# A planned attention-plus-FFN kernel: new load sizes in the planner, a new order of the first loads, value loads held to a short backlog

## The chip, the core and the metric

The kernel runs on one core of a Trainium2 chip. The metric is device time in microseconds (us) of one launch; three runs of the kernel before took 354.30, 354.94 and 356.14 us, median 354.94. The profile shows one execution of its own (354.98 us, of which 353.2 us is the span that the profile covers) at a granted TensorE clock of 1.00.

## What is computed

Attention over 8 batches, 12 heads, 448 positions of 64 values, with q and k normalised, and then a feed-forward block on the 3584 resulting rows of 768:

```
q_n, k_n = rmsnorm(q, g_q), rmsnorm(k, g_k)
attn     = softmax(q_n @ k_n.T / sqrt(64))          # 448 x 448 per head
x        = (attn @ v), heads side by side           # 3584 x 768
a, b     = x @ w1, x @ w2                           # 3584 x 1024 each
out      = ((a * b) @ w3) @ w_out                   # 3584 x 768, float32
```

All inputs are float32 in DRAM. The weights are not normalised or gated further, so w3 @ w_out can be multiplied once, ahead of use.

## The kernel before

**Work units.** The unit of attention is a quad: four heads of one batch, 24 in all (`i` = 0 to 23, three to a batch). For each quad:

- q and k are loaded (two transfers of 448 KB; quads 1 to 5 on GpSimd's queue, the others on SyncE's), squared on ScalarE (L455), summed on VectorE (L462), turned into a scale on ScalarE (L471, L474) and scaled to bf16 on VectorE (L485). Quads 0 to 4 are then transposed on TensorE (L1112), the others by DMA transposes from SyncE (L552).
- Seven score steps (L670) of four matmuls each go to two PSUM banks; each is followed by one exponential on ScalarE (L692), which writes the `P` or `Pr` tile. A planned order never has more than two scores waiting for their exponential.
- The values are loaded by four small GpSimd transfers (L399, 64 and 48 KB), and the products with them (L736, L757), together with products with ones for the softmax sum, are done for two quads at a time where possible ("pair") or for one ("single"). ScalarE makes the reciprocal (L779, L780), VectorE scales into `xT` (L799).

The feed-forward part works in "pairs": two PSUM banks, two halves of the contraction on the two row halves of the array. The w3·w_out product is 8 such pairs (128 passes of four 64x64 matmuls, 384 columns), w1 and w2 are 64 pairs (768 passes, 448 columns), the last product is 27 pairs (432 passes, 384 columns) and a shorter tail (L1053). All of these are issued at one line, L857. In the middle of each pair the two row halves swap banks, and an empty instruction (L841) on GpSimd, or early on SyncE, carries the wait for that: the pair's second half can start only when the queue of that engine has reached it.

**How the order is made.** Nothing is scheduled on the chip. When the kernel is built, class `Planner` plays the work through, with a duration in us for each piece, and emits every engine's instructions in the order that came out. At run time each engine takes its instructions strictly in that order, and waits for data where it must. What the change touches in this planner:

- *The loads.* A transfer has a size in us (`moves=(work, weight)`): two queues, SyncE's and GpSimd's, are played as sharing the DMA engines by weight, each finishing its transfers in turn. 0.7 us (`AFTER`) is added for a landing, and `LATE` more after 75 us.
- *`plan.moving["SP"]`*: what SyncE's queue still has to move at 2.3 us, for quad 0's q and k.
- *`POOL_ORDER`*: the order of the first 27 loads on GpSimd's queue: `w` is a 128-row slab of w3 (512 KB read), `o` a quarter of w_out, `q` a quad's q and k, `v` a quad's values (four transfers), `a` and `b` a third of w1 and w2 (1 MB read).
- *`quiet()`*: holds a quad's value load back while the load queue has more than `QUIET` us left, unless its scores are due.
- *`PARTS`*: in how many steps of the contraction the first three w3·w_out pairs alternate between their sides (each step needs only the quarters of w_out that have come).
- *`HOLD`*: with 1, a pair product with the values isn't started while a feed-forward pair is open and no other is ready. *`STOCK`* and *`PACE`*: with that many feed-forward pairs waiting, scores are spaced by 1.7 us.
- Where TensorE would idle before 13 us, the planner puts matmuls on zeros (L1182, 256 columns) [...].

Of the kernel before, what the change touches and what calls it, by code (L numbers as in the profile page):

```python
# [19 lines left out]
INF = float("inf")  # L20
# [4 lines left out]
LAG = {"ACT": 0.11, "DVE": 0.09, "SP": 0.0, "POOL": 0.0}  # L25
AHEAD = {"SP": 2.0, "POOL": 1.6}
AFTER = 0.7
LATE = 1.0
BUSY = 75.0


# [164 lines left out]
def kernel(  # L196
# [48 lines left out]
    MARGIN = 0.25  # L245
    LOW = 2
    PV_BANKS = 6
    HOLD = 1
    SOON = 0
    STARVED = 4  # L250
    HUNGRY = 0.6
    ONE = 0
    PARTS = ((4, 8), (4, 8), (4, 8))
    EARLY_PAIRS = 3
    AHEAD_W3 = 4
    EARLY = 4
    STOCK = 18
    PACE = 1.7
    POOL_ORDER = (
        "w0 o0 o1 w1 w2 o2 o3 q1 v0 w3 w4 q2 v1 a0 w5 w6 a1 v2 w7 v3 q3 a2 q4 b0 b1 q5 b2".split()  # L260
    )
    ON_POOL = (1, 2, 3, 4, 5)
    IN_PARTS = (6, 7, 8)
    QUIET = 0.5

    w1s = const.tile([128, CM, DFF], BF, name="w1s")
    w2s = const.tile([128, CM, DFF], BF, name="w2s")
# [46 lines left out]
    plan = Planner()  # L314
# [27 lines left out]
    def put(where, key):  # L342
        def done(t):
            where[key] = t

        return done
# [23 lines left out]
    def plan_load_qk(i, key=None):  # L370
        eng, queue = (nc.gpsimd, "POOL") if i in ON_POOL else (nc.sync, "SP")
        parts = 2 if i in IN_PARTS else 1
        for which in range(2):
            got = []

            def done(t, which=which, got=got):
                got.append(t)
                landed[i]["qk"[which]] = all_of(got, parts)

            for n in range(parts):  # L380
                x0, x1 = 2 * n // parts, 2 * (n + 1) // parts
                add(
                    queue, {"SP": 0.4, "POOL": 0.75}[queue],
                    (QUAD * i - 30 if key is None else key) + which * 0.01 + n * 0.001,
                    lambda which=which, x0=x0, x1=x1: load_qk(i, which, eng, x0, x1),
                    needs=[lambda: qk_free[i % 3] + (1.0 if i > 5 else 0.0)],
                    done=done, moves=(1.4 / parts, 0.086),
                )

    def load_v(i, z):  # L390
# [15 lines left out]
    def plan_load_v(i, key):  # L406
        got = []

        def done(t):
            got.append(t)  # L410
            if len(got) == 4:
                landed[i]["v"] = max(got)

        def quiet():

            late = i <= 3 or next_score[0] >= i * NU - 3
            return 0.0 if late or sum(x[1] for x in plan.moving["SP"]) < QUIET else INF

        for z in range(4):
            add(  # L420
                "POOL", 0.62, key + z * 0.01, lambda z=z: load_v(i, z),
                needs=[lambda: v_free[i % 4] + (3.0 if i > 3 else 0.0), quiet], done=done,
                moves=((0.48, 0.06), (0.40, 0.05))[z % 2],
            )

    def load_w12(dst, src, m):
# [860 lines left out]
    with tc.manual_schedule():  # L1287
        nc.vector.memset(warm_t, 0.0)
        nc.vector.memset(eps_t, 64e-6)
        nc.vector.memset(ones, 1.0)  # L1290
        nc.vector.memset(ones[HP:NP, 1], 0.0)
        nc.vector.memset(ones[0:HP, 2], 0.0)
        nc.vector.memset(ones_row, 1.0)
        for which in range(2):
            load_qk(0, which, nc.sync, 0, 1)
            load_qk(0, which, nc.scalar, 1, 2)
        nc.scalar.dma_start(out=g_row[:, 0], in_=g_q.unsqueeze(0))
        nc.scalar.dma_start(out=g_row[:, 1], in_=g_k.unsqueeze(0))
        nc.scalar.preload_act_table_set("natural_log_exp_and_others")
        make_identity(nc, ident)  # L1300
        for t_sb in v_bufs:
            nc.gpsimd.memset(t_sb[:, :, NF, :], 0.0)  # L1302
        def warm(n):
            for _ in range(n):
                nc.tensor.matmul(
                    out=ps_all[:, 7, :], lhsT=warm_t[:, 0:128], rhs=warm_t,
                    start=True, stop=True,
                )

        def g_product():  # L1310
            nc.vector.scalar_tensor_tensor(
                out=gp_row,
                in0=g_row[:, 0].unsqueeze(1).broadcast_to([1, 2, D]),
                scalar=8.0,
                in1=g_row[:, 1].unsqueeze(1).broadcast_to([1, 2, D]),
                op0=MULT, op1=MULT,
            )
            nc.tensor.matmul(
                out=ps_all[:, 6, 0:D], lhsT=ones_row, rhs=gp_row[:, 0],
                start=True, stop=True,  # L1320
            )
            nc.tensor.matmul(
                out=ps_all[:, 6, D : D + 1],
                lhsT=gp_row.rearrange("a x d -> a (x d)"), rhs=ones_row[:, 0:1],
                start=True, stop=True,
            )
            warm(1)

        def spread():
            nc.vector.tensor_copy(out=g_b, in_=ps_all[:, 6, 0:D])  # L1330
            nc.vector.tensor_copy(out=g_col, in_=ps_all[:, 6, D : D + 1])

        warm(WARM)
        free.update(ACT=4.0, DVE=4.0, SP=4.0, POOL=2.3, PE=7.2)
        plan.now = plan.moved_to = 2.2
        plan.moving["SP"].append([2.3, 2.6, lambda t: None, 0.086])
        landed[0].update(q=4.5, k=5.4)
        bank_at[6] = INF
        add(
            "DVE", 0.13, -13.0, g_product, needs=[lambda: 5.8], done=put(consts_at, "gp")  # L1340
        )
        add(
            "DVE", 0.22, -11.0, spread, needs=[lambda: consts_at["gp"] + 0.6],
            done=lambda t: consts_at.update(g=t + SEM) or bank_at.__setitem__(6, t + SEM),
        )
        for i in range(3):
            plan_prep(i)

        seq = [0]

        def weight(emit, moves, done):
            add("POOL", 0.6, -100.0 + seq[0], emit, done=done, moves=moves)

        for name in POOL_ORDER:
            what, x = name[0], int(name[1])
            seq[0] += 1
            if what == "o":
                weight(lambda x=x: load_wout(x), (2.15, 0.135), put(w_at["w_out"], x))
            elif what == "w":
                weight(lambda x=x: load_w3(x), (1.38, 0.172), put(w_at["w3"], x))  # L1360
            elif what == "v":
                plan_load_v(x, -100.0 + seq[0])
            elif what == "q":
                plan_load_qk(x, -100.0 + seq[0])
            else:
                dst, src, key = (w1s, moe_w1, "w1") if what == "a" else (w2s, moe_w2, "w2")
                weight(
                    lambda dst=dst, src=src, x=x: load_w12(dst, src, x), (2.6, 0.323),
                    put(w_at[key], x),
                )  # L1370
        waiting.extend(w34_pair(fc) for fc in range(CF))
        plan.run(pe_step, finished)
        if PLAN_OUT is not None:
            PLAN_OUT.append(dict(free))
# [28 lines left out]
```

## Time and profile before

| what | value |
|---|---|
| time, median of 3 | 354.94 us |
| span of the profiled execution | 353.2 us |
| TensorE (PE) matmuls | 7370, busy 98% of the span |
| ScalarE (ACT) | busy 261.1 us, 74% |
| VectorE (DVE) | busy 206.5 us, 58% |
| GpSimd (POOL) | busy 76.8 us, nearly all of it issuing transfers |
| DMA | 55.11 MB, mean 156 GB/s |

How to read it: "busy" of TensorE counts each matmul from issue to the end of its drain, and four small matmuls run side by side, so a row of the group list with a mean of 349 ns doesn't mean that one matmul follows the other after 349 ns. What counts is the distance from start to start, which the chain of waits and the timeline give: 14 passes of four matmuls in 2.65 us, 0.189 us each. In the last 70 us TensorE alone works: ScalarE and VectorE fall to two tenths, so whatever moves the end has to move TensorE's stream.

### The profile page before, as it was taken

What the parts mean: (1) busy time and instruction counts of PE and PEld (TensorE: products, weight loads), DVE (VectorE), ACT (ScalarE), POOL (GpSimd) and SP (SyncE); (2) the same over time, 40 slices, a digit from 0 to 9 for tenths busy, and PEclk for the clock granted to TensorE, in tenths of its full rate; (3) what the DMA queues carried; (4) which work ended last, traced back from release to release, by engine and by line L of the source; (5) the groups of instructions that cost most, each with busy time, mean ns of one, the idle gap of its engine ahead of it and who ended that gap; (6) DMA issues with size and microseconds to landing.
All of it is one profiled execution on the core that took longest, in us unless ns stands there. A gap on an engine that the chain in (4) does not pass through costs nothing.

```text
span 353.2 us, 16174 instructions
## 1 busy us (share of the span) xinstructions
PE 344.5 (98%) x7370; PEld 220.8 (63%) x7370; DVE 206.5 (58%) x292; ACT 261.1 (74%) x376; POOL 76.8 (22%) x134
## 2 busy tenths in 40 slices
PE   8899999999999999999999999999999999999995
PEld 4566756666665666667666565665656567666674
DVE  5359478897979487987767696576344320122200
ACT  5569979979989999999998999695979612222132
POOL 8365722211220403032032240230400000000000
PEclk9999999999999999999999999999999999999999
DMA  8999999598998999998999889783580005100046
GB/s 189 233 270 189 212 254 297 136 186 203 196 241 175 197 159 246 196 201 171 212 232 207 158 127 256 189 94 56 91 153 2 4 2 136 48 4 2 10 132 178
DMA packets 68488, 55.11 MB, mean 156 GB/s; under 512 B 45060, under 2 KB 62372, under 8 KB 68420
## 3 DMA queue, kind: packets, MB, share of 16 engines
q1 hardware_dynamic: 49440, 35.33, 44.7%
q0 software_dynamic: 18048, 16.92, 28.3%
q10 hardware_dynamic: 932, 1.84, 1.5%
q8 instruction: 57, 0.93, 1.1%
q14 instruction: 11, 0.09, 0.1%
HBM read 46.66 MB, written 11.01 MB: 163 GB/s over the span
## 4 chain that ended last, share of the span: by engine, by line
PE 87%; ACT 6%; DMA 2%; POOL 2%; issue 2%; DVE 1%; POOLq 0%; SPq 0%; ACTq 0%
PE ps_all L857 62%; PE ps_all L757 12%; PE ps_all L670 8%; ACT P L692 3%; PE ps_all L736 2%; DMA w_outs<-in_moe_w_out_dram 2%; ACT half L692 1%; POOL v_sb L399 1%; PE ps_all L1112 1%; PE ps_all L1053 1%; ACT Pr L692 1%; PE ps_all L1182 0%; DVE abT L938 0%; ACT qkT L350 0%; POOL v_sb L1302 0%
## 5 line engine op out<-in xcount | busy, mean ns | idle before, releaser
L692 ACT ACTIVATE P<-ps_all 128x896 bf16<-128x896 f32 x114 | 99.1, 922 | 9.7 <-PE ps_all L670 9.6
L399 POOL DMA_DIRECT2D v_sb<-in_v_dram x96 | 57.2, 609 | 176.8 <-PE ps_all L670 84.6
L857 PE MATMUL ps_all<-xT,w1s 64*64 64x448 bf16 x1536 | 89.4, 349 | 0.0
L857 PE MATMUL ps_all<-xT,w2s 64*64 64x448 bf16 x1536 | 88.0, 349 | 0.4 <-POOLq L841 0.4
L857 PE MATMUL ps_all<-w34s,abT 64*64 64x384 bf16 x1728 | 80.5, 323 | 0.1
L350 ACT ACTIVATE half<-ps_all 128x896 bf16<-128x896 f32 (+1 forms) x40 | 34.8, 869 | 56.1 <-PE ps_all L857 56.1
L938 DVE TENSOR_TENSOR abT<-ps_all,half 128x896 bf16<-128x896 f32 x32 | 34.8, 1089 | 57.3 <-PE ps_all L857 56.8
L857 PEld LDWEIGHTS <-abT 64*64 64x64 bf16 x1728 | 52.2, 107 | 19.6 <-POOLq L841 0.5
L857 PEld LDWEIGHTS <-w2s 64*64 64x64 bf16 x1536 | 47.6, 107 | 25.3 <-POOLq L841 0.8
L857 PEld LDWEIGHTS <-w1s 64*64 64x64 bf16 x1536 | 46.1, 107 | 25.5 <-issue 0.2
L670 PE MATMUL ps_all<-qkT 64*64 64x448 bf16 x672 | 60.9, 352 | 0.9 <-ACT P L692 0.4
L462 DVE TENSOR_REDUCE ssq<-sq 128x14 f32<-128x896 f32 (+1 forms) x50 | 51.2, 1041 | 13.9 <-ACT sq L455 13.9
L485 DVE TENSOR_TENSOR qks<-qk_sb,al 128x448 bf16<-128x448 f32 x96 | 55.5, 617 | 1.4 <-ACT al L474 1.1
L455 ACT ACTIVATE sq<-qk_sb 128x896 f32<-128x896 f32 (+1 forms) x50 | 45.3, 917 | 1.6 <-DMA qk_sb<-in_q_dram 1.5
L799 DVE TENSOR_TENSOR xT<-ps_all,r 128x448 bf16<-128x448 f32 x48 | 27.4, 617 | 12.7 <-ACT r L780 10.1
L670 PEld LDWEIGHTS <-qkT 64*64 64x64 bf16 x672 | 21.7, 106 | 14.9 <-issue 5.1
L857 PE MATMUL ps_all<-w_outs,w3T 64*64 64x384 bf16 x512 | 24.9, 324 | 1.6 <-DMA w_outs<-in_moe_w_out_dram 1.0
L692 ACT ACTIVATE w_outs<-ps_all 128x896 bf16<-128x896 f32 x24 | 21.5, 915 | 5.3 <-PE ps_all L670 5.1
L757 PE MATMUL ps_all<-P,v_sb 128*32 128x448 bf16 x456 | 25.0, 352 | 0.0
L692 ACT ACTIVATE Pr<-ps_all 128x896 bf16<-128x896 f32 x24 | 22.3, 929 | 1.7 <-PE ps_all L670 1.6
L757 PEld LDWEIGHTS <-v_sb 128*32 128x32 bf16 x592 | 15.8, 97 | 12.2
L356 DVE COPY half<-ps_all 128x768 f32<-128x768 f32 x9 | 8.6, 956 | 22.0 <-PE ps_all L857 14.0
(66 smaller groups left out, 214.8 us busy)
## 6 DMA issues: line engine op xcount, KB each, us to landing
out_dram<-half SPq DMA_DIRECT2D x48, 192.0 KB, 3.5
qk_sb<-in_q_dram SPq DMA_DIRECT2D x15, 448.0 KB, 5.3
qk_sb<-in_k_dram SPq DMA_DIRECT2D x15, 448.0 KB, 5.8
v_sb<-in_v_dram POOLq DMA_DIRECT2D x48, 64.0 KB, 3.9
v_sb<-in_v_dram POOLq DMA_DIRECT2D x48, 48.0 KB, 4.2
qk_sb<-in_q_dram POOLq DMA_DIRECT2D x5, 448.0 KB, 8.3
qk_sb<-in_k_dram POOLq DMA_DIRECT2D x5, 448.0 KB, 10.1
w3s<-in_moe_w_dram POOLq DMA_DIRECT2D x8, 256.0 KB, 7.5
```

What stands on the lines that cost most here:

```text
L350: nc.scalar.activation(out=out, in_=in_, func=AF.Copy, scale=1.0 if by is None else by)
L356: nc.vector.tensor_copy(out=out, in_=in_)
L399: nc.gpsimd.dma_start(out=v_bufs[i % 4][p0 : p0 + HP, g::2, 0 : j1 - j0].rearrange("p h j d -> p h (j d)"), in_=src[:, g::2, j0:j1].rearra ...
L455: nc.scalar.activation(out=s["sq", t][:, x0:x1], in_=src[:, t, x0:x1], func=AF.Square)
L462: nc.vector.tensor_reduce(out=s["ssq"][:, t, x0:x1], in_=s["sq", t][:, x0:x1], axis=AX, op=ADD)
L485: nc.vector.tensor_tensor(out=s["qks"][:, t, :, x], in0=src[:, t, x], in1=s["alpha"][:, t, x].unsqueeze(2).broadcast_to([NP, NJ, D]), op=MULT,
L670: nc.tensor.matmul(out=sc[HP * c : HP * c + HP, u, 0:S].rearrange("p (j s) -> p j s", j=NJ), lhsT=qkT[u * D : (u + 1) * D, 1, j, cols], rh ...
L692: lambda: nc.scalar.activation(out=dst, in_=sc[:, :, 0:S], func=AF.Exp),
L757: nc.tensor.matmul(out=ps_all[hd * HALF : (hd + 1) * HALF, z, 0:S], lhsT=value_weights(i, hd, j, kind), rhs=s["P"][:, hd, j, :] if j < NF ...
L799: lambda: nc.vector.tensor_tensor(out=xT[b][:, 2 * m + kind - 1, :], in0=ps, in1=s["r"], op=MULT),
L857: mm = nc.tensor.matmul(out=ps_all[64 * h : 64 * h + 64, p.bank + z, 0 : p.n], lhsT=lhsT[64 * r : 64 * r + 64, 64 * h : 64 * h + 64], rhs= ...
L938: nc.vector.tensor_tensor(out=abT[bp][:, f0 : f0 + 2, odd * S : (odd + 1) * S], in0=ps_all[:, z : z + 2, 0:S], in1=a_sb[b, f0], op=MULT,)
```

## The change

The planner's load sizes are set to other values (w_out 2.15 to 1.95, w3 1.38 to 1.27, w1/w2 2.6 to 2.7, q and k 1.40 to 1.35, values 0.48/0.40 to 0.28/0.24, what is left of quad 0's at the start 2.6 to 3.5), the added lateness after 75 us falls from 1.0 to 0.3 us, the first loads get another order (a quarter of w_out first, w3's slabs earlier, w1 later), and a value load now waits for both queues to be short, GpSimd's own as well as SyncE's, so that values go out a few at a time. Three settings of the planner change with it. The intent is an order that fits when data arrives. What is computed is the same, and so are the instructions of the work itself; only their order, and the number of matmuls on zeros, differ.

```diff
-LATE = 1.0
+LATE = 0.3
...
-    HOLD = 1
+    HOLD = 0
...
-    PARTS = ((4, 8), (4, 8), (4, 8))
+    PARTS = ((2, 4, 8), (4, 8), (4, 8))
...
-    STOCK = 18
+    STOCK = 14
...
-        "w0 o0 o1 w1 w2 o2 o3 q1 v0 w3 w4 q2 v1 a0 w5 w6 a1 v2 w7 v3 q3 a2 q4 b0 b1 q5 b2".split()
+        "o0 w0 w1 w2 o1 o2 o3 q1 v0 w3 w4 w5 q2 v1 v2 w6 w7 a0 a1 v3 a2 q3 q4 b0 b1 q5 b2".split()
...
-    QUIET = 0.5
+    FIRST = 3.5
+    QUIET = 1.0
...
-                    done=done, moves=(1.4 / parts, 0.086),
+                    done=done, moves=(1.35 / parts, 0.086),
...
-            return 0.0 if late or sum(x[1] for x in plan.moving["SP"]) < QUIET else INF
+            left = [sum(x[1] for x in plan.moving[e]) for e in ("SP", "POOL")]
+            return 0.0 if late or max(left) < QUIET else INF
...
-                moves=((0.48, 0.06), (0.40, 0.05))[z % 2],
+                moves=((0.28, 0.06), (0.24, 0.05))[z % 2],
...
-        plan.moving["SP"].append([2.3, 2.6, lambda t: None, 0.086])
+        plan.moving["SP"].append([2.3, FIRST, lambda t: None, 0.086])
...
-                weight(lambda x=x: load_wout(x), (2.15, 0.135), put(w_at["w_out"], x))
+                weight(lambda x=x: load_wout(x), (1.95, 0.135), put(w_at["w_out"], x))
-                weight(lambda x=x: load_w3(x), (1.38, 0.172), put(w_at["w3"], x))
+                weight(lambda x=x: load_w3(x), (1.27, 0.172), put(w_at["w3"], x))
-                    lambda dst=dst, src=src, x=x: load_w12(dst, src, x), (2.6, 0.323),
+                    lambda dst=dst, src=src, x=x: load_w12(dst, src, x), (2.7, 0.323),
```

## Prediction

> **What bounds the kernel now.** I read the page first, its engines and its slices.
>
> ```profile
> PE 344.5 (98%) x7370; PEld 220.8 (63%) x7370; DVE 206.5 (58%) x292; ACT 261.1 (74%) x376; POOL 76.8 (22%) x134
> ...
> PE   8899999999999999999999999999999999999995
> ...
> ACT  5569979979989999999998999695979612222132
> ```
>
> TensorE never rests, and after about 280 us ScalarE is down to two tenths. So the end moves only if TensorE's stream gets shorter or waits less. How much waiting is in it? Busy time doesn't tell, since small matmuls overlap. I priced the stream from starts, with two lines of the chain of waits:
>
> ```profile
> 191.34 2.65 PE ps_all L857 x56
> ...
> 281.60 63.44 PE ps_all L857 x1424
> ```
>
> The first is 14 passes of four matmuls, 0.189 us each; 384-column passes take 0.1625 by the same reading. The stream: 768 passes of w1/w2 145.3, 432 of the last product 70.2, 128 of w3·w_out 20.8, 168 of scores 31.8, value products 49.2 (864 matmuls on whole rows at 0.189 per four, 288 on half rows at 0.69 per 24), 134 transposes at 0.056 7.5, tail 2.6, 18 matmuls on zeros at 0.109 2.0: about 329.3. To this come 66 changes between kinds of matmul (0.09 each beyond the normal step: 5.9). From 7.2 us, where the work starts, that ends at 342.5; the last matmul really ends at 349.4. **So TensorE waits 6.9 us in all**, and that is everything an order can win. Counting the stream up to each value product and comparing with its start in the chain (24.3, 44.7, 75.2, 277.3 us and so on), 3.0 are lost before the first (24.2 us), 0.6 more to the second (44.7), 0.6 to 75, 2.2 to 277, 0.5 in the tail.
>
> The waits of TensorE and its timeline say on what:
>
> ```profile
> PE ps_all L857 <- DMA w_outs<-in_moe_w_out_dram: 1.0, 1, 1.0
> PE ps_all L670 <- ACT P L692: 0.4, 2, 0.2
> PE ps_all L670 <- ACT Pr L692: 0.4, 1, 0.4
> PE ps_all L857 <- POOLq L841: 0.4, 1, 0.4
> ```
>
> ```profile
> 8.56 0.56 PE L1112 MATMUL ps_all<-ident,qks 128*128 128x128 bf16 x7
> 10.14 0.52 PE L857 MATMUL ps_all<-w_outs,w3T 64*64 64x384 bf16 x8 [1.01 <-DMA w_outs<-in_moe_w_out_dram]
> ...
> 118.10 0.38 PE L670 MATMUL ps_all<-qkT 64*64 64x448 bf16 x4 [0.23 <-ACT P L692]
> ...
> 118.91 0.38 PE L670 MATMUL ps_all<-qkT 64*64 64x448 bf16 x4 [0.43 <-ACT Pr L692]
> ...
> 205.05 3.58 POOL L399 DMA_DIRECT2D v_sb<-in_v_dram  x6 [2.03 <-issue]
> ...
> 207.21 1.33 PE L857 MATMUL ps_all<-xT,w2s 64*64 64x448 bf16 x24 [0.40 <-POOLq L841]
> ...
> 345.13 1.12 PEld L857 LDWEIGHTS <-abT 64*64 64x64 bf16 x32 [0.50 <-POOLq L841]
> ```
>
> (Each shown gap is about 0.17 short of the lost time, since the drain of the matmul before counts as busy.) The first quarter of w_out came 1.0 us after the order wanted it. At 118 four scores stand in a row and wait for exponentials. At 207 the swap instruction sat in GpSimd's queue behind six value loads. At 345 the last pair has no partner to fill its swap.
>
> **What the Trainium skill says.** "TensorE: Matmul & The Clock Gate", Back-to-back issue gap, gives N/2.4 + 2.5 ns from start to start: 189 and 162.5 ns; the trace agrees (0.189). "Perfetto Trace Analysis", Identifying the Most-Contended Engine, warns that matmul busy time is no measure of headroom; here 98% hides 6.9 us. "DMA: Bandwidth & Descriptors", Issuing engines are not separate DMA queues: transfers from all engines interleave on the same 16. The trace agrees: beside quad 0's loads from SyncE and ScalarE (landed by 5.4 us) GpSimd's first two landed only at 7.0 and 10.1, later ones come 1.25 (w3) and 1.87 us (w_out) apart. Same page, Anatomy of one DMA: about 2.0 us of fixed time; the fastest value loads here land 2.2 us after issue.
>
> **The change, part by part.** The built order has the same 1536 + 1536 + 1728 + 672 + 512 + 888 work matmuls and the same 11 pair and 2 single products, so no work goes away. Zeros rise from 18 to 22 (+0.44), changes of kind fall from 66 to 63 (-0.27): counted, the new stream ends at 342.6 against 342.5. The rest is waits.
>
> *Start (load order, sizes, FIRST, PARTS).* Landings in the trace before: w0 6.97, o0 10.10, o1 11.98, w1 13.23, w2 14.52, o2 16.37, o3 18.26, q1/k1 21.00, v0 21.96, w3 23.18. The old planner expected the first ones earlier and the later ones late (2.15 for a w_out quarter that takes 1.87). Re-timed in the new order by those steps: o0 about 8.2, w0 10.1, w1 11.35, w2 12.6, o1 14.5, o2 16.4, o3 18.3, v0 unchanged. The new TensorE order, counted: first w3 transposes at 10.3 (in time), the second at 10.9 (0.45 late), the third at 12.75 (in time). With o0 alone 8 passes can run (PARTS gives the first pair four of them); the ninth falls at 14.6, o2 is wanted at 18, o3 at 19: all in time. Lone pair halves before the first value product cost 0.5 before (0.26 + 0.27) and I keep that. Loss 1.0 (0.5 to 2.0) for 3.0; the first value product at 22.3 instead of 24.2, with v0 there when needed.
>
> *22 to 45.* The new order does 16 more w3·w_out passes here (2.6 us that no longer follow the second value product). Scores of quads 1 and 2 start later, about 31.4 instead of 28.4, and 13.3 us of stream stand between them and the second value product; ScalarE has 14 x 0.83 + about 1.5 = 13.1 us in it. That just fits. Loss 0.7 (0.3 to 1.5) for 0.6.
>
> *45 to 75.* The queue delivers the same bytes, so b2 lands near 61.6 as before. The new order runs the first w2 half in one piece (24 matmuls) where the old stopped after 16; its last 8 fall at about 62.4. Quad 3's transposes stand together at about 52, and its q and k (43.0 and 44.1 before) come behind a2 now, near 46 and 47. Squares, sums and scaling take 5 us: up to 1 us of wait. Loss 1.1 (0.3 to 2.5) for 0.6.
>
> *75 to 280.* Before, one run of four scores (lost 1.0) and the GpSimd queue at 207 and 216 (0.8) are the main losses. The new order has no run of four but two of three; the third can't start before the first's exponential is done, 0.6 each. The longest run of value loads ahead of a swap falls from nine to seven, at 0.60 us each 4.2 for 5.4 us. What waits behind them is the swap, and TensorE behind it; this is the one wait the change could still leave. Fewer loads at once cost nothing, since a quad's values land many us before their product. LATE and the smaller sizes move q, k and transposes' uses up to 0.7 us earlier. ScalarE waited only 1.5 us in all for q and k before, so most of that is slack. Loss 1.8 (1.0 to 4.0) for 2.2.
>
> HOLD, STOCK and PACE only choose which ready piece TensorE takes next; what they cost or bring is already in the counted order, at nothing but these waits.
>
> *Tail.* Twelve halves of the last product follow the last w2 half, so six pairs can go two by two and none stands alone: 0.2 for 0.5.
>
> Sum: 342.6 + 1.0 + 0.7 + 1.1 + 1.8 + 0.2 = 347.4 against 349.4: **2.0 us less**, 354.94 - 2.0 = 352.9.
>
> **Rivals.** (1) *Better throughout*: every stage at its lower end (2.1 us of waits): 344.7, so 4.7 less, 350.2. For it: only data and swaps are waited for. Against: two planned score runs. (2) *The start's gain is taken back*: ScalarE, 9.28 of 10 us busy between 30 and 40, fixes the second value product, and late quad 3 and b2 eat the rest: waits 6.5, 349.1, 354.6. (3) *Slower*: the planner now believes in landings that come later. If 0.4 of the 0.7 us taken from LATE reaches TensorE for 10 of the 15 quads loaded after 75 us, that is 4 us, on top of the main sum 351.4: 356.9. For it: loads of q and k took 3.3 to 7.2 us from issue to landing there, a wide spread. Against: the 1.5 us.
>
> **How the numbers follow.** Main case 0.47, rival 1 0.12, rival 2 0.23, rival 3 0.18. The likeliest is 352.9. The range takes in rival 1 and rival 3 and is open a little at both: 349.6 to 357.2. Faster by over 0.5% means under 353.17: rival 1 and most of the main case, 0.53. Slower, above 356.7: most of rival 3 and a little else, 0.18. The same: 0.29.
>
> **What would show it.** Right: no wait for w_out at 10 us, first value product near 22.3, the second with all w3·w_out done near 45.6; no wait for POOLq over 0.3 us between 75 and 280; no half alone at the end. Wrong: waits for DMA on q, k or transposes after 75 us; a stop near 52 or 62 us over 1 us; three-score runs that cost over 1 us each.

## The result, and the profile after

| | before | after |
|---|---|---|
| time, median (lowest to highest) | 355.5 us (354.3 to 356.1, 6 runs) | 358.6 us (357.4 to 361.5, 6 runs) |
| span of the profiled run | 353.2 us | 358.3 us |
| TensorE's last end in it | 349.4 us | 354.3 us |

The kernel after takes 1.010 of the time of before (95% interval 1.0057 to 1.0144): 3 us more, where 2 us less were predicted. It was profiled twice (the second time is called e9 below), and the two profiles differ: TensorE ends at 354.3 in the first, of a 360.1 us execution, and at 352.5 in the second, of a 358.6 us execution, which is the more typical one.

The page of the first, its engines and two of its slices:

```profile
PE 346.2 (97%) x7374; PEld 235.0 (66%) x7374; DVE 208.3 (58%) x294; ACT 261.2 (73%) x374; POOL 76.7 (21%) x134
...
PE   8998899999999999999999999999999999999995
...
ACT  4776797999999999988789898776696933222122
```

TensorE is as full as before and ScalarE as empty after 280 us, so again only TensorE's own stream and its waits can have moved the end. The stream didn't. From the chain of waits of after:

```profile
240.99 1.89 PE ps_all L859 x40
...
292.44 59.05 PE ps_all L859 x1336
```

Ten passes of four matmuls in 1.89 us are 0.189 each, as before, and the same work ends at the same counted 342.6 us. So TensorE waits 354.3 - 342.6 = 11.7 us in the first profile and 9.9 in the second, against 6.9 before; the prediction had 4.8. (Line numbers in after are one or two higher: L857 is L859 here, L670 L672, L455 L457.) TensorE's waits in the first profile:

```profile
PE ps_all L1136 <- DMA w3s<-in_moe_w_dram: 1.9, 3, 1.0
PE ps_all L1307 <- DVE warm_t L1290: 1.2, 1, 1.2
PE ps_all L859 <- issue: 1.2, 2, 0.9
PE ps_all L738 <- ACT w_outs L694: 0.7, 2, 0.4
PE ps_all L672 <- ACT qkT L351: 0.7, 1, 0.7
PE ps_all L672 <- ACT P L694: 0.7, 1, 0.7
```

The w_out wait of before is gone (the L1307 line is the warm-up at 1 us, in every profile). In its place stand the transposes of w3, 1.9 us; "issue", a stop for which the profile shows no releaser; and scores that waited for ScalarE. Where the first and the last of these come from shows in ScalarE's and GpSimd's rows. ScalarE's waits for q and k, before and then after:

```profile
ACT sq L455 <- DMA qk_sb<-in_q_dram: 1.5, 3, 0.7
```

```profile
ACT sq L457 <- DMA qk_sb<-in_q_dram: 4.0, 3, 2.5
ACT sq L457 <- DMA qk_sb<-in_k_dram: 3.5, 4, 2.0
```

1.5 us have become 7.5. L457 computes the squares of a quad; everything behind it in ScalarE's order, exponentials too, waits along. But when these waits fall matters, since LATE acts only after 75 us. Before that time they are 5.1 us (1.2 in the kernel before), most of it in two places, quad 1's q and quad 2's k:

```profile
20.32 0.95 ACT L457 ACTIVATE sq<-qk_sb 128x896 f32<-128x896 f32 x1 [2.53 <-DMA qk_sb<-in_q_dram]
...
30.29 0.95 ACT L457 ACTIVATE sq<-qk_sb 128x896 f32<-128x896 f32 x1 [2.00 <-DMA qk_sb<-in_k_dram]
```

From 75 us on they are 2.4 us in this profile and 3.7 in the second, against 0.3 before. Now the timeline of after between 30 and 38 us, GpSimd and TensorE:

```profile
30.55 0.59 POOL L400 DMA_DIRECT2D v_sb<-in_v_dram  x1 [2.36 <-DMA qk_sb<-in_k_dram]
31.14 1.12 POOL L435 DMA_DIRECT2D w3s<-in_moe_w_dram  x2
...
35.74 0.62 PE L1136 MATMUL ps_all<-ident,w3s 128*128 128x128 bf16 x8 [0.61 <-DMA w3s<-in_moe_w_dram]
...
37.31 0.62 PE L1136 MATMUL ps_all<-ident,w3s 128*128 128x128 bf16 x8 [0.95 <-DMA w3s<-in_moe_w_dram]
```

GpSimd wants to issue the last of the eight value loads of quads 1 and 2 and stands for 2.36 us, until quad 2's k has landed at 30.3. That k is the eighth transfer back: in this stretch none of GpSimd's transfers is issued before the one eight back has landed. The last two slabs of w3 stand behind the value loads, are issued at 31.1 and 31.7 and land at 35.7 and 37.3. In between there was next to nothing to move: the 16 transfer engines were busy to 0.16 from 30 to 32 us, after being fully busy from 28 to 30.

### The profile page after: what moved, and what is told of

The parts are those of the page before. It is cut to its first block, busy times and chain, and to the rows that moved or that the text cites. A ratio compares the mean times of both kernels' runs of the same rounds, so it can differ in the third digit from the quotient of the medians.

```text
span 358.3 us, 16174 instructions
## 1 busy us (share of the span) xinstructions
PE 346.2 (97%) x7374; PEld 235.0 (66%) x7374; DVE 208.3 (58%) x294; ACT 261.2 (73%) x374; POOL 76.7 (21%) x134
## 4 chain that ended last, share of the span: by engine, by line
PE 74%; DMA 10%; ACT 8%; DVE 3%; issue 2%; POOL 1%; SPq 0%; POOLq 0%; DVEq 0%
PE ps_all L859 53%; PE ps_all L759 10%; PE ps_all L672 7%; DMA qk_sb<-in_k_dram 6%; ACT P L694 4%; PE ps_all L738 2%; ACT sq L457 2%; DMA w_outs<-in_moe_w_out_dram 2%; DMA w3s<-in_moe_w_dram 2%; DMA qk_sb<-in_q_dram 1%; DVE qks L487 1%; ACT w_outs L694 1%; PE ps_all L1055 1%; ACT Pr L694 1%; DVE half L357 1%
## 5 line engine op out<-in xcount | busy, mean ns | idle before, releaser
L694 ACT ACTIVATE P<-ps_all 128x896 bf16<-128x896 f32 x108 | 93.9, 918 | 12.5 <-PE ps_all L672 12.0
L859 PE MATMUL ps_all<-xT,w1s 64*64 64x448 bf16 x1536 | 91.3, 349 | 1.5 <-issue 1.2
L859 PE MATMUL ps_all<-xT,w2s 64*64 64x448 bf16 x1536 | 91.0, 349 | 0.2
L859 PE MATMUL ps_all<-w34s,abT 64*64 64x384 bf16 x1728 | 79.6, 323 | 0.0
L351 ACT ACTIVATE half<-ps_all 128x896 bf16<-128x896 f32 (+1 forms) x38 | 32.8, 864 | 51.6 <-PE ps_all L859 51.6
L859 PEld LDWEIGHTS <-w1s 64*64 64x64 bf16 x1536 | 53.0, 107 | 21.7 <-issue 1.8
L859 PEld LDWEIGHTS <-w2s 64*64 64x64 bf16 x1536 | 54.0, 107 | 20.0 <-issue 1.2
L940 DVE TENSOR_TENSOR abT<-ps_all,half 128x896 bf16<-128x896 f32 x32 | 34.8, 1089 | 54.6 <-PE ps_all L859 54.2
L859 PEld LDWEIGHTS <-abT 64*64 64x64 bf16 x1728 | 54.5, 107 | 17.4
L672 PE MATMUL ps_all<-qkT 64*64 64x448 bf16 x672 | 64.1, 352 | 1.7 <-ACT qkT L351 0.7
L457 ACT ACTIVATE sq<-qk_sb 128x896 f32<-128x896 f32 (+1 forms) x50 | 45.3, 922 | 7.7 <-DMA qk_sb<-in_q_dram 4.0
L672 PEld LDWEIGHTS <-qkT 64*64 64x64 bf16 x672 | 25.4, 106 | 16.2 <-issue 7.3
L694 ACT ACTIVATE w_outs<-ps_all 128x896 bf16<-128x896 f32 x30 | 26.8, 914 | 3.5 <-PE ps_all L672 3.2
L859 PE MATMUL ps_all<-w_outs,w3T 64*64 64x384 bf16 x512 | 25.1, 324 | 0.2
L694 ACT ACTIVATE Pr<-ps_all 128x896 bf16<-128x896 f32 x24 | 22.2, 926 | 1.2 <-PE ps_all L672 1.2
L357 DVE CAST half<-ps_all 128x896 bf16<-128x896 f32 x13 | 14.2, 1090 | 12.3 <-PE ps_all L859 11.9
```

Of the source, the lines that this page charges most:

```text
L351: nc.scalar.activation(out=out, in_=in_, func=AF.Copy, scale=1.0 if by is None else by)
L357: nc.vector.tensor_copy(out=out, in_=in_)
L457: nc.scalar.activation(out=s["sq", t][:, x0:x1], in_=src[:, t, x0:x1], func=AF.Square)
L672: nc.tensor.matmul(out=sc[HP * c : HP * c + HP, u, 0:S].rearrange("p (j s) -> p j s", j=NJ), lhsT=qkT[u * D : (u + 1) * D, 1, j, cols], rh ...
L694: lambda: nc.scalar.activation(out=dst, in_=sc[:, :, 0:S], func=AF.Exp),
L859: mm = nc.tensor.matmul(out=ps_all[64 * h : 64 * h + 64, p.bank + z, 0 : p.n], lhsT=lhsT[64 * r : 64 * r + 64, 64 * h : 64 * h + 64], rhs= ...
```

## The experiments

Each run was timed against the kernel before on the same chip. "Loss" is what TensorE lost beyond its counted stream in a stretch, worked out as in the prediction: the start of the value product at the stretch's end less the counted start, for each order its own (they end at 342.3 to 342.6). Losses, ScalarE's waits for q and k, and TensorE's stops with no releaser ("issue") are each from one profile; the ratio is from the timed runs. The column "no stops" is the loss from 75 to 280 us less the stops in it; PV is a value product.

```
run                      loss, us                                    ScalarE's waits   stops    ratio to before
                         to 1st  to 2nd  to 75   to 280  no     sum  for q and k       "issue"  (95% interval)
                         PV      PV                      stops  to end  to 75  from 75
before                   3.0     0.6     0.5     2.3     2.3     6.9    1.2    0.3     0
same order, 5 more       2.2-3.4 0.6     0.6-1.6 1.9-2.9 1.9-2.4 6.1-9.1 1.3-2.8 0-0.6 0-1.5
after                    0.7     3.6     1.8     5.3     4.1    11.7    5.1    2.4     1.2      1.0100 (1.0057-1.0144)
e9 after again           1.2     1.3     2.1     5.0     4.8     9.9    2.6    3.7     0.4      1.0103 (1.0048-1.0158)
e1 after, w3 first       1.1     1.3     2.2     4.7     4.7     9.6    3.3    2.4     0.3      1.0062 (1.0038-1.0086)
e2 after, LATE 1.0       0.6     1.4     2.0     5.1     2.9     9.4    1.5    2.0     2.2      1.0027 (1.0004-1.0049)
e8 e1 and e2 together    1.0     0.7     2.6     3.1     2.8     7.7    1.5    0.8     1.1      1.0025 (0.9996-1.0053)
e3 after, half values    0.6     1.4     2.4     2.8     2.6     7.5    3.1    0.6     0.6      1.0025 (1.0002-1.0048)
e4 before, half values   3.1     0.5     0.5     1.3     1.3     5.9    1.3    0       0        0.9965 (0.9943-0.9986)
e5 before, LATE 0.3      2.5     0.9     0.5     3.6     3.6     7.6    1.5    3.5     0        1.0038 (1.0023-1.0052)
e7 before, new start     0.9     1.6     2.2     3.8     3.1     8.8    2.6    3.9     0.7      1.0043 (1.0021-1.0065)
e6 before, 2 ns          2.1     1.5     0.7     4.3     4.0     8.8    3.3    0.3     0.3      1.0044 (1.0028-1.0060)
e12 before, stores apart 3.2     0.6     1.1     2.1     1.5     7.4    1.5    1.0     0.6      0.9995 (0.9977-1.0012)
```

The second row shows how much one order varies from execution to execution. Its five profiles come from the runs e10, e11 and e13 to e15 below, which follow the order of before up to 302 us. The sum moves by 3 us and the stretch from 45 to 75 us by 1 us, so a small difference between two single profiles says little there; the column "no stops" moves by only 0.5 us.

**e1: the last slabs of w3 ahead of quad 2's values.** The order stays; only which load GpSimd's eight slots carry changes.

```diff
+        slots = jobs_of["v2"] + jobs_of["w6"] + jobs_of["w7"]
+        emits = [j.emit for n in ("w6", "w7", "v2") for j in jobs_of[n]]
+        for job, emit in zip(slots, emits):
+            job.emit = emit
```

> The changed kernel, every engine's order as it is, except that in GpSimd's queue the last two slabs of w3 (w6, w7) go out ahead of the four value loads of quad 2 instead of behind them. Theory 'the queue runs dry' (eight small value loads use up the eight transfers that may be in flight, the slabs behind them are issued 2 us late and TensorE's transposes wait at 35 to 37 us): the waits for w3 there fall from 1.9 us to under 0.3 and the time from 358.6 to 356.3 to 357.2. Rival 'the start is set by ScalarE': the waits move to the exponentials, the second value product stays near 48.2 us, and the time stays at 358.6 within 0.7.

TensorE's waits of this run, the line for w3:

```profile
PE ps_all L1136 <- DMA w3s<-in_moe_w_dram: 0.4, 1, 0.4
```

The two slabs landed at 32.2 and 33.5 in place of 35.7 and 37.3, and TensorE no longer waited for them: the 0.4 that is left falls at 11 us, at another slab. So the value loads in front of w3 did hold it up. The time, 358.0 us, missed the expected 356.3 to 357.2. 1.0062 against 1.0100 is 1.3 us, but the two intervals overlap a little, and after itself, profiled again (e9), waited 1.0 us for w3 and lost no more before the second value product than this run. With LATE at 1.0 the same exchange brought nothing (e8 below, 1.0025 for 1.0027). The edit mends a real wait of about 1 us; what that is worth in time is not shown, and most of the loss is elsewhere.

**e2: LATE back to 1.0 in the kernel after.**

```diff
-LATE = 0.3
+LATE = 1.0
```

> The changed kernel with LATE back at 1.0, planned anew; its order differs from the changed kernel's only a little, GpSimd's and SyncE's not at all. Theory 'LATE is not it': 358.6 within 1. Rival of the prediction (the planner's belief in earlier landings after 75 us costs up to 4 us): 355 to 356.5.

2.6 us of time came back (1.0027). GpSimd's and SyncE's orders are the same as in after, and ScalarE's and TensorE's are the same up to 157 and 160 us; so what e2 gained in the early waits (1.5 for 5.1 us up to 75 us) is not LATE's doing but differs from execution to execution. What LATE changes shows from 157 us on, for instance at 184 us, in ScalarE's timeline of after and then of e2:

```profile
181.52 1.73 ACT L694 ACTIVATE w_outs<-ps_all 128x896 bf16<-128x896 f32 x2 [0.25 <-PE ps_all L672]
184.14 0.95 ACT L457 ACTIVATE sq<-qk_sb 128x896 f32<-128x896 f32 x1 [0.90 <-DMA qk_sb<-in_q_dram]
185.00 0.90 ACT L694 ACTIVATE w_outs<-ps_all 128x896 bf16<-128x896 f32 x1
```

```profile
181.25 2.57 ACT L694 ACTIVATE w_outs<-ps_all 128x896 bf16<-128x896 f32 x3 [0.25 <-PE ps_all L672]
183.71 0.94 ACT L457 ACTIVATE sq<-qk_sb 128x896 f32<-128x896 f32 x1
```

With LATE 0.3 the squares stand behind two exponentials and wait 0.90 us for their q, and the third exponential waits with them. With LATE 1.0 the third exponential goes first, and the squares find their data there. TensorE's loss from 75 to 280 us without stops is 4.1, 4.8 and 4.7 us in the three profiles with LATE 0.3 (after, e9, e1) and 2.9 and 2.8 in the two with 1.0 (e2, e8). The profile of e2 had one bad stop of its own, 2.2 us at 93, of which more below.

**e3 and e4: no value loads for quads 12 to 23**, in the kernel after and in the one before. This leaves out half of v's transfers; the products take what lies in the buffers.

```diff
     def load_v(i, z):
+        if i >= 12:
+            return
```

> The changed kernel in its own order, but the value loads of quads 12 to 23 are left out (the products read old values, so the output is wrong there). Theory 'value loads in GpSimd's queue and on the DMA engines cause the late loss': from 150 us on, TensorE loses 0.5 to 1 us instead of about 2.8, 356.3 to 357.2. Rival 'SyncE's own queue, stores ahead of q, k and transposes': at most 0.7 less, 357.9 to 358.9.

> The kernel before in its own order, with the value loads of quads 12 to 23 left out in the same way (output wrong there). Theory 'value loads': its smaller late loss of about 1.2 us falls to 0.4, 354.5 to 355. Rival 'SyncE's queue': 355.5 within 0.4.

Without them after is 0.75% faster and before 0.35%, as the first theory had it for both. So the late value loads cost something in both, and more in after, where the loss from 75 to 280 us fell from 5.0 or more to 2.8 and ScalarE's waits for q and k from 75 us on from 2.4 or more to 0.6. That fits value loads that delay the loads of q and k beside them, in an order that has less slack for it: without them LATE 0.3 costs no more than LATE 1.0 with them (e2). The swap behind a row of value loads is a small part of it. No matmul of after waits 0.3 us or more for POOLq, but two weight loads do (PEld; the other one at 270 us, 0.55):

```profile
210.53 0.90 PEld L859 LDWEIGHTS <-w2s 64*64 64x64 bf16 x24 [0.54 <-POOLq L843]
```

TensorE's matmuls start 0.48 us apart there in place of 0.189, about 0.3 us lost at each place.

**e5: LATE 0.3 alone, in the kernel before.**

> The kernel before with LATE 0.3 in place of 1.0 and nothing else; the order differs from about 100 us on. Theory 'LATE costs' (my rival 3: q, k and transposes are believed to come 0.7 us earlier than they do, and TensorE pays): undoing it in the kernel after brought 0.73%, so here it should cost as much: 1.007 of before, 358.3 us, and the trace shows more waits of TensorE for scores or exponentials whose quad came late. Theory 'order by luck' (a changed constant mainly deals another order, and the believed lateness itself hardly matters): within 0.3%, 354.7 to 356.9.

1.0038, between the two expectations. ScalarE's waits for q and k rose from 1.5 us to these 4.9, and nearly all of the rise falls after 75 us (3.5 for 0.3):

```profile
ACT sq L455 <- DMA qk_sb<-in_q_dram: 3.3, 3, 1.9
ACT sq L455 <- DMA qk_sb<-in_k_dram: 1.6, 2, 1.0
```

The loss from 75 to 280 us grew by 1.3 us (3.6 for 2.3; the five further profiles of before's order have 1.9 to 2.4 without stops), as much as the time. So LATE 0.3 loses 1.2 to 2.0 us there in after's order and 1.2 to 1.7 in before's. These are two pairs of orders, not three: e1 and e8 have the orders of after and e2, but for GpSimd's loads.

**e6: a change that says nothing.** DRAIN, the planner's 0.110 us for the drain of a matmul, becomes 0.112 in the kernel before.

> The kernel before with DRAIN 0.112 in place of 0.110: the planner believes 2 ns more for one drain of TensorE, which says nothing new of the chip, but another order comes out from about 15 us on. Theory 'order by luck': the order of before is a chosen good one, and an order dealt at random is worse by as much as the kernel after is, 1.005 to 1.015, 357.5 to 361. Theory 'the change itself costs' (the order matters little as long as the beliefs are the same): 0.997 to 1.003, 354.7 to 356.9.

1.0044: as much as LATE alone or the new start alone. A 2 ns change deals another order from about 15 us on, and that order is 1.6 us worse than the one of before. Its waits are not those of LATE: ScalarE waits 0.3 us for q and k from 75 us on, as in before, but value products wait 1.2 us for VectorE. It is one such change; how wide the spread of orders is was not measured.

**e7: the new start alone**, in the kernel before: the new order and sizes of GpSimd's loads, FIRST, and PARTS.

> The kernel before with the part for the start alone: the new order of GpSimd's loads, their new sizes, FIRST 3.5 and the first entry of PARTS; LATE, HOLD, STOCK, PACE, the value loads' sizes and the rule for them stay. First value product at 22 to 23 us in place of 24.2 by every theory. Theory 'the queue runs dry behind the value loads': the fifth to eighth quarter of w3 come 2 to 3 us late as in the kernel after, the second value product falls at 47 or later, and nothing of the start's gain is left: 1.003 to 1.012, 357 to 360. Theory 'the start was good and the rest of the change is what costs': the gain of 1.5 to 2 us holds to the end: 0.994 to 0.997, 353.7 to 354.7.

First value product at 22.2, as predicted: 2.1 us of loss saved. Then every stretch loses more than before, 1.0, 1.7 and 1.5 us more, and the gain is gone by 75 us. The last two slabs of w3 landed at 34.8 and 36.1, but TensorE's waits show only 0.3 us for them, and ScalarE waits 6.6 us for q and k, 3.9 of it from 75 us on, with LATE still at 1.0. So a low LATE is not the only thing that puts squares ahead of their data, and the start alone loses by the whole order that it leads to; the dry queue is a small part of it.

**e8: e1 and e2 together.**

> The kernel after with both edits that helped alone: the last two quarters of w3 issued ahead of quad 2's value loads (1.0062 of before, against 1.010 for the kernel after), and LATE 1.0 (1.0027). If they mend different waits they add: 0.999, 355.4 us, second value product at 45.5 to 46.5. If both mend the same thing or LATE helped by another order only, no better than the better one: 1.0025 to 1.006, 356.7 to 358.

1.0025: no better than LATE alone, and not told apart from before. The two edits don't add up to what each brought alone. With both, the second value product is at 45.6, the predicted time, the loss before it 0.7, as predicted, and the loss from 75 to 280 us is 3.1 for 4.7 in e1.

**e9: the kernel after once more.**

> The kernel after, unchanged, for a second profile of it beside these runs. Theory 'order and beliefs decide' (the waits belong to the order): the same stalls as in its first profile, in order of time w3 at 35 and 37 us, scores at 121, the stop without a releaser at 226, TensorE's last end within 0.7 us of 354.3; time 1.010 of before. Theory 'small shifts in the transfers decide where TensorE stops': the planned ones stay (121 us, 0.8), the others move or vanish by over 1 us in sum; time between 1.003 and 1.010.

The same ratio, and other waits: the w3 stops fell from 1.9 to 1.0 us, the stop at 226 from 0.9 to 0.2, and a new one came. ScalarE's and TensorE's timelines around 158 us:

```profile
157.37 0.95 ACT L457 ACTIVATE sq<-qk_sb 128x896 f32<-128x896 f32 x1 [2.07 <-DMA qk_sb<-in_q_dram]
...
158.69 0.90 ACT L694 ACTIVATE P<-ps_all 128x896 bf16<-128x896 f32 x1
```

```profile
159.64 0.38 PE L672 MATMUL ps_all<-qkT 64*64 64x448 bf16 x4 [1.34 <-ACT P L694]
```

This is rival 3 of the prediction at work: q, issued at 151.6, took 5.7 us; ScalarE stood 2.07 us before its squares, the exponential queued behind them came late, and the scores that wanted its bank waited 1.34 us. In the first profile the squares of the same quad waited 0.61, for k at 160, and TensorE not at all; there it was scores at 187 that waited 0.32, behind the squares at 184 shown above. The run of three scores at about 121 cost 0.84 us in both. So the places that wait belong to the order; how long they wait changes from execution to execution.

**e12: stores kept away from loads.** The kernel before, with a rule for the planner that holds output stores back while SyncE has 0.8 us of transfers outstanding, and three constants (STOCK 14, QUIET 0.8, EARLY_PAIRS 4) picked for the shortest planned end.

```diff
+    def room():
+        return 0.0 if sum(x[1] for x in plan.moving["SP"]) < 0.8 else INF
...
-                        needs=[lambda: e + SEM], moves=(0.55, 0.14),
+                        needs=[lambda: e + SEM, room], moves=(0.55, 0.14),
```

> The kernel before with one rule more for the planner: an output store is not issued while more than 0.8 us of SyncE's transfers are outstanding, so that stores don't pile up on loads of q and k; with STOCK 14, QUIET 0.8 and EARLY_PAIRS 4, chosen among some thousand sets for the shortest planned end. Theory 'a plan that waits less and a shorter backlog both hold on the chip': no stop of TensorE without a releaser, 0.6 us less than before, 0.997 to 0.999, 354.3 to 355.2. Theory 'order by luck' (waits that the planner doesn't see decide): 1.000 to 1.008, 355.5 to 358.5.

0.9995: no measurable gain, though the interval doesn't exclude the 0.6 us that were expected. One stop without a releaser, 0.6 us, came where none was expected. By this run a better plan by the planner's own reckoning need not be a better kernel at this level.

### The stops with no releaser

**e10 and e11: twelve plain loads at 302 us, six and two deep.** Between 302 and 334 us TensorE does matmuls that wait for nothing, and the transfer engines rest; the loads go into dead buffers.

```diff
             def store_then_loads(x):
                 store(x)
                 stores[0] += 1
                 if stores[0] == 42:
+                    for tile, which in [(z, w) for z in range(3) for w in range(2)] * 2:
+                        load_qk(tile, which, nc.sync)
```

> The kernel before with twelve loads of q and k (448 KB each) added on SyncE at about 302 us, into the three dead q/k buffers, so that up to six are under way at once; nothing reads them and no engine waits for them, the rest of the order is unchanged, and TensorE does nothing but the last product there. Theory 'TensorE's own instructions come through the same DMA engines and queue behind what is there': in the profiles so far the instruction transfer that was due 5.7 us earlier left TensorE without work for about 1.0 us, and 6.7 us for 2.4; six loads at some 1.4 us each make a delay of 5 to 8 us for two or three transfers: stops of 1 to 3 us each with no releaser between 303 and 325 us, 2 to 6 us in all, 357.5 to 361. Theory 'the stops with no releaser have another cause': nobody waits, 354.5 to 356.5, and the stretch from 302 to 330 has no stop.

> The same twelve loads at the same place, all into one q/k buffer, so that each pair waits for the pair before it and two are under way at most: the same bytes over a somewhat longer stretch. Theory 'the instructions queue behind the backlog': a delay of at most 3 us, no stop, within 0.3% of before. Theory 'loads slow TensorE by their traffic, whatever their number under way': a loss like that of the six-deep run.

(What TensorE does there is w1 and w2, not the last product.) No stop in either: 0.9998 (0.9973 to 1.0023) and 1.0019 (1.0005 to 1.0034), and from 302 to 334 us TensorE ran through. The burst delayed the instruction transfers by 2.7 to 3.1 us with six loads under way (1.3 to 2.4 with two), which was not enough to tell.

**e13, e14, e15: the mixture seen at the stops**, three times (transpose, q, k, two stores, transpose, two stores), then the same without the transposes, then without the stores.

> The kernel before with 24 transfers added on SyncE at about 302 us, in the mixture of the stretches where TensorE stopped: three times (transpose, q, k, two output stores, transpose, two output stores), into dead buffers and into output rows that are written later. Six plain loads deep (the run before this) delayed TensorE's instruction transfers by 2.7 to 3.1 us only, and no stop came. Theory 'late instructions stop TensorE, and it takes the mixture to make them late': delays of over 4.5 us for one or two of the three transfers due between 303 and 320, one or two stops with no releaser, 0.5 to 2.5 us each, and none where the delay is under 4; 355.8 to 359. Theory 'the stops have another cause': no stop from 302 to 330 whatever the delay.

> The same without the transposes: three times (q, k, four output stores), 18 transfers. Theory 'the transposes make the instructions late' (small packets, 256 bytes, that hold the transfer engines): delays as in the six-deep burst, about 3 us, no stop, within 0.3% of before. Theory 'it is the sum of what is under way': delays of 4 to 6 us, a stop of 0.5 to 2 us.

> The same without the stores: three times (transpose, q, k, transpose), 12 transfers. Theory 'the transposes make the instructions late': delays over 4.5 us and a stop, as in the mixed burst. Theory 'it is the sum of what is under way': delays of 3 us or less, since SyncE takes 1.3 us for each transpose and so less piles up, no stop.

Again no stop after 302 us (0.9990, 1.0015 and 1.0008, all with 1 inside the interval). The greatest delays there were 3.0, 4.2 and 2.3 us. So SyncE's traffic alone did not make the instructions late enough, whatever its kind; my theory of what makes them late fell.

But these five kernels are the kernel before up to 302 us, so with the first profile there are six profiles of one order, and they settle the other half. Instructions come in by a queue of their own, on the page of before and after alike:

```profile
q8 instruction: 57, 0.93, 1.1%
```

57 transfers of 16 KB are 0.93 MB. "Trainium Architecture — The Big Picture" of the Trainium skill, The software stack, has instructions of 64 bytes, which for TensorE's 2 x 7370 (each matmul has a weight load) makes 0.94 MB: as good as all of them. The same place says that the streams are moved in when the program is loaded; here they are moved while it runs, one transfer about every 256 instructions. Each can be given a time at which it is due, 256 instructions after the one before. (The count starts at the same instruction in all six profiles, so the differences below hold whatever its zero is.) For the transfer due at 44 to 45 us:

```
run     due     landed   TensorE's instructions     stop after the 11th of
                         from due to landing        24 matmuls at about 50 us
e11     43.9    48.6     218                        none
before  44.7    49.6     229                        none
e15     44.7    50.0     253                        0.30, goes on at 51.32
e10     44.2    49.5     253                        0.38, goes on at 50.86
e13     44.1    49.9     269                        0.92, goes on at 51.38
e14     45.1    51.1     277                        0.92, goes on at 52.37
```

TensorE's timeline there, before and then in e13:

```profile
50.31 1.45 PE L857 MATMUL ps_all<-xT,w1s 64*64 64x448 bf16 x24
```

```profile
49.72 0.73 PE L857 MATMUL ps_all<-xT,w1s 64*64 64x448 bf16 x11
51.38 0.91 PE L857 MATMUL ps_all<-xT,w1s 64*64 64x448 bf16 x13 [0.92 <-issue]
```

The same program stops at the same instruction or doesn't, by how late its transfer is, and goes on 1.3 to 1.5 us after the landing. The stops of the other orders fit: in after, whose timeline at 226 us and e2's at 95 follow, the transfers landed at 226.06 and 93.85, when TensorE had 3 instructions and none left before the place where it stopped (e14: 3, e13: 11, e10 and e15: 27).

```profile
225.99 0.55 PE L859 MATMUL ps_all<-xT,w1s 64*64 64x448 bf16 x7
227.43 0.35 PE L859 MATMUL ps_all<-xT,w1s 64*64 64x448 bf16 x1 [0.89 <-issue]
```

```profile
95.32 0.38 PE L859 MATMUL ps_all<-xT,w1s 64*64 64x448 bf16 x3 [2.21 <-issue]
```

Counted in TensorE's recorded instructions, all 19 stops that the 17 profiles show lie whole multiples of 256 apart, to within 16 of over 7000, in whatever order: e1, e3, e8 and e9, with other work there, stop at the same instruction as these six (the 1723rd to 1725th), and TensorE goes on 1.2 to 1.6 us after a landing every time. So "issue" ahead of TensorE is, in all these places, TensorE out of instructions. The six profiles of before's order have 0 to 1.5 us of it (e14 has 0.6 more at 219), the two of after 1.2 and 0.4. It makes single executions differ; it does not explain the 1%.

## Why the prediction was wrong

The same losses by the steps of the prediction:

```
stretch      predicted   after   after again (e9)
to 1st PV    1.0         0.7     1.2
22 to 45     0.7         3.6     1.3
45 to 75     1.1         1.8     2.1
75 to 280    1.8         5.3     5.0
tail         0.2         0.3     0.3
sum          4.8         11.7    9.9
```

One reading of the prediction first. The formula that it takes from "TensorE: Matmul & The Clock Gate" of the Trainium skill, Back-to-back issue gap, is there the gap of a matmul by itself; for a stream with weight loads the page gives other figures (131 ns at 512 columns). The measurement decides: 0.189 us for a pass of four 448-column matmuls. And the second line of the chain that it shows mixes both widths; 384-column passes start 0.163 us apart in the last 13 us of before, so its figure stands.

**Start: right.** No wait for w_out; six passes had run when its second quarter landed at 13.9 us; first value product at 22.0 and 22.5 for 22.3:

```profile
11.85 0.50 PE L859 MATMUL ps_all<-w_outs,w3T 64*64 64x384 bf16 x8
...
22.03 0.75 PE L759 MATMUL ps_all<-P,ones 128*32 128x448 bf16 x12
```

**22 to 45: right in the typical execution, short of a term in the worst.** I re-timed GpSimd's transfers one behind the other as if its queue never ran dry. It did: eight small value loads used up the eight places under way, and GpSimd could not issue the large loads behind them in time. 0.7 became 3.6 in the first profile, where q and k of quads 1 and 2 came late besides, and 1.3 to 1.4 in the three others with the same orders up to there (e9, e2, e3), inside the range of 0.3 to 1.5; with the loads exchanged it is 1.3 (e1) and 0.7 (e8).

**45 to 75: within its range** (0.3 to 2.5), at its upper half, and by luck: no wait of TensorE of 0.2 us or more is for quad 3's q and k or for b2, on which the 1.1 us rested. What shows is 0.4 us of a value product that waits for an exponential, just before 78 us in the first profile, and a stop of 0.2 near 50 in the second. The rest is not explained.

**75 to 280: the step that failed, by 3.3 us.** "Most of that is slack" was said of LATE, because ScalarE had waited only 1.5 us for q and k before. Of these 1.5 us only 0.3 fall after 75 us, so they said little about the stretch where LATE acts. There the planner, with LATE 1.0, had kept squares behind other work until their data were there (e2 at 184 us). With 0.3 they move forward in ScalarE's order, ScalarE waits 2.4 and 3.7 us from 75 us on, and scores wait behind the exponentials behind the squares. Rival 3 had the mechanism, but at 4 us for TensorE it was too high: undoing LATE takes 1.2 to 2.0 us off the loss without stops. I put rival 3 at 0.18 against a wait that the change itself would make. In time e5 and e2 price LATE at 0.38% and 0.73% (1.3 and 2.6 us), in the second case most of what after lost. Whether it is the belief alone is not settled: e6 shows that another order dealt by 2 ns costs 0.44% too, though by other waits, and e7 has 3.9 us of ScalarE's waits with LATE 1.0. The second part missing in this step are the stops with no releaser, which I had as nothing: 1.2 us in one profile of after and 0.2 in the other. With LATE 1.0 and without stops 2.8 and 2.9 us are left against the 1.8. In it, three scores in a row cost 0.84 for the estimated 0.6, at one place and not two, and two swaps behind value loads, the wait that the prediction left open, about 0.3 each.

**Tail: right.** The last product runs through without a lone half:

```profile
336.68 14.81 PE L859 MATMUL ps_all<-w34s,abT 64*64 64x384 bf16 x360
351.42 2.83 PE L1055 MATMUL ps_all<-w34s,abT 128*64 128x192 bf16 x64
```

**Behind all steps: the order of before was not an average order.** I took its 6.9 us of waits as what an order has, and looked for what the change would take away. e6 shows that a change of no meaning gives away 1.6 us; e5 and e7, each one part of the change, give away 1.3 and 1.5; only e12, picked among many for its planned end, gives away nothing. A new order should have been expected to wait more unless the profile said why not.

What stays open: how much of the 1% is LATE's belief and how much is merely another order; why e8, with both faults mended and a start that is 2 us earlier, still doesn't beat before (1.0025, 1 just inside the interval), and what makes TensorE's instruction transfers later than 4.3 us, which the bursts on SyncE did not reach. At the places with stops, loads of values or of w2 from GpSimd, or q, k, stores and transposes together, were under way.

## What to carry to other kernels

An engine's small waits under a planned order are made by the plan: before a due time is taken tighter, look for what the old one kept out of the way of other work, here exponentials behind squares that wait for a load. When loads are put in a new order, count how many may be under way at once, since a row of small ones can use up the places and leave the transfer engines idle while a large one waits to be issued. And measure what a change of no meaning does to a planned order before giving a part of the change the credit or the blame: here it was 0.44%, as much as either part alone. Before a wait is put down to a setting, look whether it falls where the setting can act: most of ScalarE's waits that set the first profile of after apart from before fell ahead of 75 us, where LATE does nothing, and more than half of them were gone in a second profile of the same kernel.

## What the runs showed that I had not expected

In these traces TensorE's instructions come through the transfer engines while the kernel runs, 16 KB at a time, about one transfer for 256 instructions. With little else under way they start 0.1 to 0.5 us after they are due; in dense stretches 3 to 6.7 us. Up to 229 instructions from due to landing cost nothing at the place with six profiles; 253 cost 0.3 to 0.4 us, 269 and 277 cost 0.9, and TensorE goes on 1.2 to 1.6 us after the landing. The profile shows it only as "issue" within a run of matmuls that wait for nothing. And twelve loads of 448 KB each (5.5 MB), or 24 transfers of mixed kind, running beside matmuls that don't need them cost no time that could be measured in four of the runs and 0.2% in e11, whose interval leaves 1 out (e10, e11, e13 to e15).
